# Chunked attention and a two-layer MLP in one kernel: the order of the transfers of tiles 1 to 5 and of tile 8 on SyncE's queue, and the general path's transfers on GpSimd's queue

## The chip, the cores and the metric

The kernel runs on one core of one Trainium2 chip. The metric is the device time of one execution in microseconds. Before the change it is 267.47 us, the median of three runs (267.15, 267.47 and 268.73). Engines are named as in the profile: PE (TensorE matmul), PEld (TensorE weight load), DVE (VectorE), ACT (ScalarE), POOL (GpSimd) and SP (SyncE, which issues nearly all transfers). "SPq" and "POOLq" are the instructions of an engine's sequencer that count as no work of the engine: issues of transfers, semaphore waits, branches.

## What is computed

Attention inside chunks of 64 keys, for 8 batches, 8 heads, 576 positions (9 chunks) and a head size of 64, and then an MLP on the result:

```python
scores = scale * np.matmul(q_c, k_c.transpose(0, 1, 2, 4, 3))     # per chunk of 64
attn = np.exp(scores - max); attn = attn / (sum(attn) + 1e-09)
x = np.matmul(attn, v_c)                # -> 4608 tokens x 512
h = x @ w_in                            # 512 x 2048
g = 0.5 * h * (1.0 + erf(h / sqrt(2)))
out = g @ w_out                         # 2048 x 512
```

Inputs and output are float32; the kernel multiplies in bfloat16.

## The kernel before

**Tiles.** The 4608 tokens are cut into nine tiles of 512. Tiles 0 to 7 hold the first eight chunks of one batch each, tile 8 the ninth chunk of all batches. The main loop `for t in range(1, NT)` runs the MLP of tile t on PE and beside it the attention of tile n = t + 1, the scores of tile t + 2 in part, and the transfers of tiles up to t + 3. Both matrix products use a seven-product scheme (four blocks by four, with sums and differences of blocks made by DVE): `mm1_seven` / `play` for the first (PE rows L598), `mm2_seven` (L758) and `mm2_steps` (L788) for the second.

**The way of an input.** A load (`load_qk`, `load_v_rows`; rows L136, L139, L142, L145, L152) brings float32 rows into a stage buffer ("arrival", six of them). A cast (rows L189, L193, L195, L235) writes them as bfloat16 to `q_nat`, `k_nat` or `v_nat`; nearly all casts run on POOL. For queries and keys a transposing transfer follows (`flip`, L228), which the scores need (`quad_S`, PE rows L261). V goes from the cast straight to `quad_av` (PE rows L346). So the chain is load, cast, flip, scores for q and k, and load, cast, `quad_av` for V.

**The way of an output.** PE sums one block of the second product in PSUM. `keep` copies a block to one of four `y` buffers (ACT, rows "kept L718" and "kept L795"), `done` adds to it (DVE, rows L723 and L798), and `store_block` (L863) sends it out: four stores of 256 KB for a tile. A `y` buffer comes free when its store has landed.

**What sets the order.** Each engine works its instructions off in program order, and that order is written out by hand (`manual_schedule`). For t = 1 the hooks `e1` and `e2` say after which piece of the tile's work a step is put: `e2[s]` stands ahead of piece s of the second product, which has 14 pieces (0 to 13). For t = 2, 3 and 4 the lists in `STEPS` say it, step by step: LQ, LK, LV are loads of q and k of tile t + 3 and of V of tile n + 1; CQ0 to CQ3, CK0 to CK3, CV the casts of these; FQ, FK the flips of tile n + 1; AV is `quad_av` of tile n; K1, K2, K3, K6 are `keep`s with K6 also storing; D1, D4, D5 are `done` with its store; XS1 to XS4 are DVE's sums of x, P0 to P3 DVE's partial row sums; s12 and the like are DVE's additions to products of the first layer. Q8, at the end of step list 4, loads and casts the queries of tile 8. For t of 5 and more `flip_qk(n + 1)` and `next_loads` stand at the head of the tile.

**SP at tile 1.** After the loads of q and k of tile 3 the program issues on SP, in this order: loads of q and k of tile 4 (`e2[4]`), the store of block (0,0) of tile 1, the flips of q and k of tile 3 and the nine loads of V of tile 3 (`e2[7]`), the stores of blocks (1,1), (0,1) and (1,0) of tile 1, and then the first flip of step list 2.

**The general path.** The fast path leaves out the maximum of the scores. DVE checks at the end that all row sums lie in a safe range (`range_test`, `range_count`, L891); each engine loads the count (L1332) and branches (L1333). If the count falls short, `general()` computes everything again, chunk by chunk, in a loop. In this input it is not taken. The instructions of L1358 are the program's end, where SP waits for all semaphores and the engines meet.

Of the kernel before, what the change touches and what calls it, by code (L numbers as in the profile page):

```python
# [11 lines left out]
def kernel(  # L12
# [9 lines left out]
    nc = tc.nc  # L22
# [5 lines left out]
    B, H, S, D = q.shape  # L28
# [154 lines left out]
    def cast_qk(t, nm, g, copy):  # L183
        st = tiles[t]
        if nm not in st:
            st[nm] = ld.tile([P, G, J, 2, D], bf16, tag="k", name="k_nat", bufs=3)
        if nm == "k" and t >= K0:
            for q0 in range(0, G, 2):
                copy(st[nm][:, q0:q0 + 2, g], st[nm + "f"][:, 2 * q0:2 * q0 + 4, g].rearrange("p (q r) d -> p q r d", r=2))  # L189
            return  # L190
        if t > T0:
            for j in range(0, J, 2):
                copy(st[nm][:, g, j:j + 2].rearrange("p j r d -> p r j d"), st[nm + "f"][:, 2 * g:2 * g + 2, j:j + 2])  # L193
            return
        copy(st[nm][:, g].rearrange("p j r d -> p r j d"), st[nm + "f"][:, 2 * g:2 * g + 2])  # L195
# [34 lines left out]
    def cast_v_rows(t, copy):  # L230
        st = tiles[t]
        st["v"] = ld.tile([P, H, CT // 2, D], bf16, tag="v", name="v_nat")
        for r in range(2):
            for n in range(CT // 2):
                copy(st["v"][:, r::2, n], st["vf"][:, r::2, n])  # L235
# [247 lines left out]
    def mm1_slot(t, f):  # L483
# [3 lines left out]
        for ks in range(KS):  # L487
# [32 lines left out]
             3: ('xs1', 'p1', "p1''", "p1'", 's11', 'FQ', "s11''", 'p2', "p2''", 'q5', 'xs2', "q5''", 'p6', "p6''", 'c11', 'k5', 'xs3', 'FK', 's12', "q5'", "c11''", "k5''", "s12''", "p1'''", 'p4', 'LQ', "p4''", "k5'", "s11'", 'c12', "c12''", 'xs4', 'p7', 'c22+', "s11'''", "p6'", "q5'''", 'LK', 'LV', 'c22', "p7''", "s12'", "c22+''", "k5'''", "p2'", "p7'", "p2'''", "p6'''", "c11'", "p4'", 'q3', "c22''", "c11'''", "c22+'", "c22'", "q3'", 'CQ0', "c12'", 'g3', "s12'''", "p7'''", "q3''", "g3'", "p4'''", 'CQ1', "c22+'''", "q3'''", "g3''", "c22'''", "c12'''", 'Y', "g3'''", 'S1a', 'S', 'Y', 'exp', 'CQ2', 'S3', 'E2', 'S1b', 'E0', 'S2b', 'Y', 'S2a', 'E1', 'Y', 'S4a', 'S4b', 'CQ3', 'E3', 'sums', 'K1', 't1', 'AV', 'Y', 'ov1', 'Y', 'CK0', 'Y', 'D1', 'ov0', 'R1', 'X1', 'K2', 'R0', 'ov3', 'Y', 'ov2', 'X0', 'K3', 'R3', 'XS1', 'X3', 'Y', 'Y', 'S+', 'E+3', 'Y', 'E+1', 'CK1', 'Y', 'R2', 'E+0', 'D4', 'X2', 'D5', 'CK2', 'CK3', 'P1', 'XS2', 'E+2', 'Y', 'P3', 'P2', 'CV', 'Y', 'gelu', 'XS4', 'K6', 'XS3', 'P0'),  # L520
             4: ("p1''", 'FQ', 'FK', "s11''", 'LQ', 'p1', "q5''", "p2''", 'LK', "p1'", 's11', "p6''", 'p2', "k5''", "s11'", "s12''", "p2'", "q5'", 'c11', 'q5', 'LV', "c11'", 'p6', "p6'", 'k5', "k5'", "p7''", "c11''", 's12', "p4''", "s12'", 'p7', "c22+''", "p7'", 'CQ0', "c12''", 'c22+', "p4'", 'p4', 'q3', "p1'''", "c22+'", "c22''", 'g3', "q3'", "q5'''", "s11'''", "g3'", "k5'''", 'CQ1', "p6'''", 'CQ2', 'Y', "c12'", 'T0', 'c22', "p2'''", "s12'''", 'R2', 'c12', "q3''", "c22'", "p7'''", "g3''", "p4'''", 'R1', 'Y', "c22+'''", 'R3', "c11'''", "c12'''", 'S1a', "q3'''", "c22'''", 'S1b', "g3'''", 'K1', 'AV', 'S2a', 'S2b', 'CQ3', 'CK0', 'S3', 'Y', 'Y', 'Y', 'Y', 'Y', 'Y', 'S4a', 'K2', 'Y', 'D1', 'Y', 'CK1', 'X3', 'K3', 'X2', 'X1', 'exp', 'CK2', 'X0', 'S+', 'S4b', 'Y', 'XS3', 'D4', 'E+0', 'CK3', 'E+2', 'E+3', 'E+1', 'XS1', 'gelu', 'Y', 'P0', 'XS2', 'Y', 'P2', 'Y', 'CV', 'D5', 'P3', 'XS4', 'P1', 'Q8', 'K6')}
# [286 lines left out]
    def play(t, order):  # L808
# [41 lines left out]
        does["FQ"], does["FK"] = lambda: flip(n + 1, "q"), lambda: flip(n + 1, "k")  # L850
        does["LV"], does["CV"] = lambda: load_v_rows(n + 1), lambda: cast_v_rows(n + 1, PO)
# [41 lines left out]
    def general():  # L893

        SUBS = mybir.AluOpType.subtract
        for c in range(4):
            n = d_ff // 4
            raw = stage_tile()[:].rearrange("p (ks n) -> p ks n", ks=KS)
            nc.sync.dma_start(raw, w_in_v[:, :, c * n:(c + 1) * n])
            DV(w_in_sb[:, :, c * n:(c + 1) * n], raw)  # L900
        for c in range(4):
            n = FF // 4
            raw = stage_tile()[:].rearrange("p (f n) -> p f n", f=n)
            nc.sync.dma_start(raw, w_out_v[:, c * n:(c + 1) * n, :])
            DV(w_out_sb[:, c * n:(c + 1) * n, :], raw)
# [4 lines left out]
    def one_chunk(b, s0, SUBS):  # L910
        rows = bass.ds(s0, CH)
        nat = {}
        for nm, src in (("q", q), ("k", k), ("v", v)):
            raw = stage_tile()[0:CH, 0:d_model]
            nc.sync.dma_start(raw.rearrange("p (h d) -> p h d", h=H),
# [54 lines left out]
        nc.sync.dma_start(by_batch[bass.ds(b, 1), rows].rearrange("o key d -> (o key) d"), y_sb[0:CH])  # L970
# [122 lines left out]
    with tc.manual_schedule():  # L1093
# [158 lines left out]
        for t in range(1, NT):  # L1252
# [26 lines left out]
            def next_loads():  # L1279
                if t + 3 == NT - 1:  # L1280
                    load_qk(t + 3, "k")
                    pool_cast_qk(t + 3, "k")
# [16 lines left out]
            if t <= T0:  # L1299
# [10 lines left out]
                if t == 1:  # L1310
# [4 lines left out]
                    e2[4].append(lambda: [load_qk(4, nm) for nm in "qk"])  # L1315
                    e2[7] += [lambda: pool_cast_qk(4), lambda: flip_qk(3), lambda: load_v_rows(3), lambda: cast_v_rows(3, PO)]
# [46 lines left out]
```

## Time and profile before

| | |
|---|---|
| median of three runs | 267.47 us |
| the profiled execution's own time | 269.52 us |
| its span, from the first to the last instruction | 267.7 us |
| mean granted TensorE clock | 0.993 |
| PE busy (share of the span) | 256.5 us (96%) |
| DVE busy | 223.3 us (83%) |
| ACT busy | 190.4 us (71%) |
| POOL busy | 104.7 us (39%) |
| transfers of SP's queue | 53.23 MB, 78.0% of 16 DMA engines' span |

The profiled execution took 2.05 us longer than the median run, and 1.8 us of its time lie outside the span. Rows of the timeline give start and length in us, the engine, the line, the operation, output and input, how many were merged into the row, and in brackets how long the engine had been idle and what ended that. Rows of the view by line give shortest, median and longest duration in ns.

### The profile page before, as it was taken

Reading aid. Unit: us, or ns where it says so; the run is one execution under the profiler, and the core shown is the slowest. Engines: PE = TensorE matmul, PEld = TensorE weight load, DVE = VectorE, ACT = ScalarE, POOL = GpSimd, SP = SyncE. Lnnn points to the kernel's source line nnn. Section 1 sums busy time; section 2 is a strip of 40 time slices with the busy share of each in tenths; the row PEclk is TensorE's granted clock in tenths of the full one; section 3 lists DMA queues with packets and bytes.
Section 4 is the critical chain, followed back from the end, with each engine's and each line's share of the span. In section 5 each row is a group of like instructions: output and inputs, shape, how many; then the busy total and the mean of one; then the engine's idle time right before and its main releaser. Section 6 shows DMA issues by size and latency. Waiting matters only on the chain.

```text
span 267.7 us, 7854 instructions
## 1 busy us (share of the span) xinstructions
PE 256.5 (96%) x3116; PEld 211.7 (79%) x3122; DVE 223.3 (83%) x397; ACT 190.4 (71%) x386; POOL 104.7 (39%) x229
## 2 busy tenths in 40 slices
PE   6599999999999999999999999999999999999992
PEld 2378865556888888887888888898888888888881
DVE  5767786998997687678999999999999999848771
ACT  3666667987767978898887588947894788237610
POOL 7778578702375370570390094087211300000000
PEclk9979999999999999999999999999999999999999
DMA  6999998979889999989999998999963310130014
GB/s 198 259 327 399 393 402 213 288 192 284 238 223 247 185 254 254 231 221 249 279 243 207 284 211 219 184 173 210 275 150 86 123 42 2 40 120 1 2 39 122
DMA packets 123415, 54.02 MB, mean 202 GB/s; under 512 B 97776, under 2 KB 120304, under 8 KB 123376
## 3 DMA queue, kind: packets, MB, share of 16 engines
q1 hardware_dynamic: 123072, 53.23, 78.0%
q8 instruction: 25, 0.41, 0.6%
q10 hardware_dynamic: 304, 0.26, 0.3%
q14 instruction: 14, 0.11, 0.1%
HBM read 36.70 MB, written 9.44 MB: 172 GB/s over the span
## 4 chain that ended last, share of the span: by engine, by line
PE 70%; ACT 8%; SPq 7%; DMA 6%; DVE 3%; POOL 2%; issue 2%; POOLq 0%; ACTq 0%
PE hs_ps L598 23%; PE y_ps L758 18%; PE y_ps L788 9%; PE h_ps L462 5%; ACT h L606 3%; DMA arrival<-in_q_dram 3%; SPq L152 3%; SPq L136 3%; PE y_ps L1021 3%; DMA arrival<-in_k_dram 2%; ACT k_bd L219 2%; PE h_ps L478 2%; PE av_ps L346 1%; DMA out_dram<-kept 1%; PE y_ps L985 1%
## 5 line engine op out<-in xcount | busy, mean ns | idle before, releaser
L606 ACT ACTIVATE h<-hs_ps 128x512 bf16<-128x512 f32 x87 | 49.7, 610 | 6.9 <-PE hs_ps L598 6.0
L235 POOL CAST v_nat<-arrival 128x256 bf16<-128x256 f32 x56 | 25.9, 488 | 37.3 <-DMA arrival<-in_v_dram 36.8
L598 PEld LDWEIGHTS <-w_in_sb 128*128 128x128 bf16 x348 | 33.9, 98 | 4.6 <-issue 0.2
L193 POOL CAST q_nat<-arrival 128x256 bf16<-128x256 f32 x40 | 17.9, 495 | 48.3 <-DMA arrival<-in_q_dram 26.8
L598 PE MATMUL hs_ps<-x,w_in_sb 128*128 128x256 bf16 x232 | 31.7, 272 | 0.0
L758 PEld LDWEIGHTS <-h 128*128 128x128 bf16 x240 | 23.2, 98 | 2.8
L1091 ACT ACT_TABLE_LOAD x16 | 20.5, 1283 | 1.0 <-PEq L1347 0.8
L718 ACT COPY kept<-y_ps 128x512 f32<-128x512 f32 (+1 forms) x17 | 9.0, 535 | 16.0 <-PE y_ps L758 13.0
L189 POOL CAST k_nat<-arrival 128x256 bf16<-128x256 f32 x48 | 18.6, 430 | 3.2 <-DMA arrival<-in_k_dram 3.2
L758 PE MATMUL y_ps<-w_out_sb,h 128*128 128x256 bf16 x160 | 18.6, 273 | 0.0
L758 PE MATMUL y_ps<-v_bd,k_bd 128*128 128x256 bf16 x160 | 18.5, 273 | 0.1
L758 PEld LDWEIGHTS <-k_bd 128*128 128x128 bf16 x160 | 15.6, 98 | 2.1 <-issue 0.2
L615 ACT COPY hs_ps<-hs_ps 128x512 f32<-128x512 f32 x29 | 16.2, 582 | 0.6 <-PE hs_ps L598 0.5
L598 PE MATMUL hs_ps<-k_bd,w_in_sb 128*128 128x256 bf16 x116 | 16.6, 273 | 0.0
L490 ACT ACTIVATE h<-h_ps 128x512 bf16<-128x512 f32 x21 | 12.5, 604 | 5.1 <-PE h_ps L462 3.6
L269 ACT ACTIVATE pT<-s_ps 128x512 bf16<-128x512 f32 x28 | 14.4, 599 | 1.8 <-PE s_ps L261 1.8
L788 PEld LDWEIGHTS <-h 128*128 128x128 bf16 x144 | 13.8, 98 | 1.7
L598 PE MATMUL hs_ps<-k_bd,w_in_more 128*128 128x256 bf16 x96 | 14.2, 273 | 0.0
L462 PE MATMUL h_ps<-x,w_in_sb 128*128 128x256 bf16 x128 | 14.2, 273 | 0.0
L598 PEld LDWEIGHTS <-w_in_more 128*128 128x128 bf16 x128 | 12.5, 98 | 2.0 <-issue 0.3
L723 DVE TENSOR_TENSOR kept<-y_ps,kept 128x512 f32<-128x512 f32 (+1 forms) x16 | 10.4, 651 | 4.0 <-PE y_ps L758 2.3
L462 PEld LDWEIGHTS <-w_in_sb 128*128 128x128 bf16 x128 | 12.4, 98 | 1.6 <-DVE w_in_sb L1066 0.2
(174 smaller groups left out, 640.2 us busy)
## 6 DMA issues: line engine op xcount, KB each, us to landing
arrival<-in_v_dram SPq DMA_DIRECT2D x58, 128.0 KB, 3.2
arrival<-in_k_dram SPq DMA_DIRECT2D x28, 256.0 KB, 5.8
arrival<-in_q_dram SPq DMA_DIRECT2D x7, 1024.0 KB, 6.7
out_dram<-kept SPq DMA_DIRECT2D x24, 256.0 KB, 3.1
arrival<-in_moe_w_out_dram SPq DMA_DIRECT2D x4, 1024.0 KB, 12.4
arrival<-in_moe_w_in_dram SPq DMA_DIRECT2D x6, 512.0 KB, 7.9
out_dram<-y_sb SPq DMA_DIRECT2D x8, 256.0 KB, 3.1
arrival<-in_v_dram SPq DMA_DIRECT2D x28, 64.0 KB, 2.8
```

The source lines that it names most:

```text
L189: copy(st[nm][:, q0:q0 + 2, g], st[nm + "f"][:, 2 * q0:2 * q0 + 4, g].rearrange("p (q r) d -> p q r d", r=2))
L193: copy(st[nm][:, g, j:j + 2].rearrange("p j r d -> p r j d"), st[nm + "f"][:, 2 * g:2 * g + 2, j:j + 2])
L235: copy(st["v"][:, r::2, n], st["vf"][:, r::2, n])
L269: nc.scalar.activation(pT[:].rearrange("p u (c j) -> p u c j", j=J), tiles[t]["s_ps"][m // 2][m % 2][:].rearrange("p u (j c) -> p u c j", ...
L462: nc.tensor.matmul(to[:, cols], left, right[:, cols], start=(start and a == 0), stop=stop, skip_group_check=True)
L490: nc.scalar.activation(tiles[t]["h"][:, f, :], h_ps[:], Act.Gelu)
L598: nc.tensor.matmul(hs[:, f], left[:, ks, f * P:(f + 1) * P], right[:, ks], start=(fresh and f == 0 and ks == 0), stop=(ks == 1), skip_grou ...
L606: nc.scalar.activation(h[:, n:n + HM, HD * c:HD * (c + 1)], src, Act.Gelu)
L615: "s11": lambda: AC(place_of("b")[:], bank["a"][:]),
L758: nc.tensor.matmul(to, left(f, m), right[:, f], start=(fresh and (split or m == 0) and f == 0), stop=(f == HF - 1), skip_group_check=True)
L788: nc.tensor.matmul(bank[name][:, m], left(f, m), right[:, f], start=(fresh and m == 0 and f == 0), stop=(f == HF - 1), skip_group_check=True)
L1091: nc.scalar.activation(act_scratch[:], rest[:, 0:1], func)
```

## The change

- **General path.** The loads and the store of `general` and `one_chunk` are issued by GpSimd's queue instead of SP's.
- **Tile 1.** `e2[4]` loads only the queries of tile 4; `e2[7]` casts only these. The flips of tile 3, the load and cast of the keys of tile 4 and the load and cast of V of tile 3 move to `e2[12]`, behind the stores of blocks (1,1) and (0,1) of tile 1.
- **V of tile 5.** The cast (CV) leaves the end of step list 3. A new step PV, fifth in step list 4, makes it, behind a one-element write of DVE to the same tile (`after=True`), so that POOL's casts wait for DVE to get there.
- **Queries of tile 8.** Q8 goes from the end of step list 4; for t = 5 `next_loads` brings q and k of tile 8 together.
- **Casts of k.** For tiles 2 and 3 each quarter is one cast of 128x512 instead of two of 128x256.

```diff
         if nm == "k" and t >= K0:
-            for q0 in range(0, G, 2):
-                copy(st[nm][:, q0:q0 + 2, g], st[nm + "f"][:, 2 * q0:2 * q0 + 4, g].rearrange("p (q r) d -> p q r d", r=2))
+            n = 2 if t > T0 else G
+            for q0 in range(0, G, n):
+                copy(st[nm][:, q0:q0 + n, g], st[nm + "f"][:, 2 * q0:2 * (q0 + n), g].rearrange("p (q r) d -> p q r d", r=2))
             return
...
-    def cast_v_rows(t, copy):
+    def cast_v_rows(t, copy, after=False):
         st = tiles[t]
         st["v"] = ld.tile([P, H, CT // 2, D], bf16, tag="v", name="v_nat")
+        if after:
+            nc.vector.memset(st["v"][0:1, 0:1, 0, 0:1], 0.0)
...
-             3: (... 'P3', 'P2', 'CV', 'Y', 'gelu', 'XS4', 'K6', 'XS3', 'P0'),
-             4: ("p1''", 'FQ', 'FK', "s11''", 'LQ', ... 'XS4', 'P1', 'Q8', 'K6')}
+             3: (... 'P3', 'P2', 'Y', 'gelu', 'XS4', 'K6', 'XS3', 'P0'),
+             4: ("p1''", 'FQ', 'FK', "s11''", 'PV', 'LQ', ... 'XS4', 'P1', 'K6')}
...
+        does["PV"] = lambda: cast_v_rows(n, PO, True)
...
-            nc.sync.dma_start(raw, w_in_v[:, :, c * n:(c + 1) * n])
+            nc.gpsimd.dma_start(raw, w_in_v[:, :, c * n:(c + 1) * n])
...
                 if t + 3 == NT - 1:
-                    load_qk(t + 3, "k")
-                    pool_cast_qk(t + 3, "k")
+                    bring_qk(t + 3)
...
-                    e2[4].append(lambda: [load_qk(4, nm) for nm in "qk"])
-                    e2[7] += [lambda: pool_cast_qk(4), lambda: flip_qk(3), lambda: load_v_rows(3), lambda: cast_v_rows(3, PO)]
+                    e2[4].append(lambda: load_qk(4, "q"))
+                    e2[7].append(lambda: pool_cast_qk(4, "q"))
+                    e2[12] = [lambda: flip_qk(3), lambda: load_qk(4, "k"), lambda: pool_cast_qk(4, "k"),
+                              lambda: load_v_rows(3), lambda: cast_v_rows(3, PO)]
```

The other three transfers of the general path (loads of `w_out` and of q, k, v, and the store) change in the same way as the one shown.

More of the change, by code (lines that the diff above doesn't have):

```diff
@@ L969, in one_chunk @@
         by_batch = out.rearrange("(b s) d -> b s d", s=S)
-        nc.sync.dma_start(by_batch[bass.ds(b, 1), rows].rearrange("o key d -> (o key) d"), y_sb[0:CH])
+        nc.gpsimd.dma_start(by_batch[bass.ds(b, 1), rows].rearrange("o key d -> (o key) d"), y_sb[0:CH])
     def last_piece(t, m, y_ps):
```

8 lines of the change are left out of this document (4 added, 4 removed).

## The prediction

> **What bounds the kernel now.** I read the busy times first, then PE's windows, then PE's waits.
>
> ```profile
> span 267.7 us, 7854 instructions
> PE 256.5 (96%) x3116; PEld 211.7 (79%) x3122; DVE 223.3 (83%) x397; ACT 190.4 (71%) x386; POOL 104.7 (39%) x229
> ...
> 20.00:263.00 243.00, 241.72 (x2961) 1.00 0.79 199
> ...
> PE y_ps L788 <- ACT kept L795: 0.2, 1, 0.2
> ```
>
> The window from 20 to 263 us holds 241.72 us of PE work in 243.00 us, at a granted clock of 1.00. PE idles there for 243.00 − 241.72 = 1.28 us, part of it after its last product. The only wait of PE on another engine in that stretch is the last row. The change takes no product away, so what lies between 20 and 263 us can give back about 1 us at most, whatever the transfers do. Two places are left: that one wait, and the end, where PE has nothing to do:
>
> ```profile
> 262.44 0.16 PE L890 MATMUL count<-small 128*1 128x1 bf16 x1
> 262.12 1.36 SPq L977 DMA_DIRECT2D out_dram<-y_sb  x2
> ...
> L1333 SPq EVENT_SEMAPHORE  x8: 17/17/17, 265.0 to 265.5; - x8
> L1333 POOLq COMPARE_BRANCH  x2: 38/42/45, 263.6 to 263.7; - x2
> ...
> L1333 SPq COMPARE_BRANCH  x2: 38/48/57, 264.6 to 265.5; - x2
> ...
> L1358 SPq EVENT_SEMAPHORE  x10: 17/28/28, 266.1 to 267.7; - x10
> L1358 POOLq EVENT_SEMAPHORE  x4: 17/17/17, 266.7 to 267.6; - x4
> ```
>
> From PE's end to the span's end 267.7 − 262.6 = 5.1 us pass. SP is the last engine there. At L1333, the branch past the general path, it handles eight semaphores one after the other between its two branches (264.6 and 265.5); POOL, whose part of the general path issues no transfer, has its two branches 0.1 us apart and no such rows. At 266.1 SP begins the closing waits, and POOL's first closing row (266.7) follows those.
>
> **The change part by part.**
>
> *General path on POOL's queue.* I read the eight semaphores as the bookkeeping of SP's transfers in the skipped block, one for each transfer semaphore. If they go with the transfers, SP's two branches come 0.1 us apart as POOL's do now, so 0.9 − 0.1 = 0.8 us fall away. SP's last store is issued by 262.12 + 1.36 = 263.5 us, and SP waits for it in any case; the first of the eight rows stands at 265.0, so I let SP reach the closing waits no sooner than about 265.3 instead of 266.1: still 0.8. Against that, new semaphores of POOL's queue will want closing waits too. SP's closing waits are among the ten rows of L1358; a step of that kind is priced by the eight of L1333, 0.5 us from first to last, 0.07 each. Four to eight more cost 0.3 to 0.5 us. POOL itself gets the eight steps: 263.7 + 0.6 = 264.3, two microseconds before its row at 266.7, so they are hidden by SP. The term is between −0.8 + 0.3 = −0.5 and −0.8 + 0.5 = −0.3 if both parts hold, −0.8 if no closing wait comes, and +0.5 if SP keeps its eight and the closing waits come on top. I take −0.5, since POOL's present rows are the nearest case of an engine without transfers in that block.
>
> [...]
>
> *Tile 1 on SP.* The rows of SP, PE, ACT, POOL and DVE that this touches:
>
> ```profile
> 75.08 1.36 SPq L142 DMA_DIRECT2D arrival<-in_q_dram  x1
> 76.49 7.27 SPq L136 DMA_DIRECT2D arrival<-in_k_dram  x4
> 83.86 0.79 SPq L863 DMA_DIRECT2D out_dram<-kept  x1
> 84.75 3.47 SPq L228 DMA_TRANSPOSE q_t<-q_nat  x1
> 88.33 2.79 SPq L228 DMA_TRANSPOSE k_t<-k_nat  x1
> 91.17 5.21 SPq L152 DMA_DIRECT2D arrival<-in_v_dram  x9
> 96.48 1.62 SPq L863 DMA_DIRECT2D out_dram<-kept  x2
> ...
> 79.07 0.68 DVE L723 TENSOR_TENSOR kept<-y_ps,kept 128x512 f32<-128x512 f32 x1
> ...
> 100.17 0.58 ACT L795 COPY kept<-y_ps 128x512 f32<-128x512 f32 x1 [1.90 <-DMA out_dram<-kept]
> 100.81 1.91 PE L788 MATMUL y_ps<-v_bd,s_sb 128*128 128x256 bf16 x16 [0.24 <-ACT kept L795]
> 102.64 0.71 PE L346 MATMUL av_ps<-pT,v_nat 64*64 64x64 bf16 x64
> ...
> 99.05 0.83 POOL L235 CAST v_nat<-arrival 128x256 bf16<-128x256 f32 x2 [0.35 <-DMA arrival<-in_v_dram]
> ```
>
> SP issues without a pause and far behind the program: the last `done` of tile 1 ends at 79.07 + 0.68 = 79.75 us, its store goes out after 96.48. ACT's K2 at 100.17 waited 1.90 us for such a store to land, and PE 0.24 us for K2. After the change two stores stand right behind the queries of tile 4, and the third behind them: 75.08 + 1.36 + 0.79 + 0.79 is 78.0 us, and the block (0,1) is ready at 79.75. SP waits 1.7 us there, with the flips of tile 3, the keys of tile 4, V of tile 3, the last store and, through the casts, POOL behind it. Both stores are out by 80.6 us, some 16 us earlier, so K2's buffer is free: PE gains 0.24 us.
>
> What becomes late is V of tile 3, now behind the keys. The same blocks stand ahead of it as before, plus two stores (1.62), plus the wait (1.7): at most 3.3 us. Its casts end at 99.05 + 0.83 = 99.88, and PE takes it at 102.64, so 2.76 us are free; at the full 3.3 PE would stall 0.5. But SP's rows for k are long because earlier transfers are still being worked off:
>
> ```profile
> 74.19 0.85 SPq L136
> ```
>
> One of the keys' four issues takes 0.85 us when nothing holds it, 3.4 for four, where the row above has 7.27. Time that SP waits comes back there. I take no stall, and keep 0 to +0.5 for the range. The flips of tile 3 move from 84.75 to about 80.6 and their scores only gain. At 98.7 SP begins step list 2 as before, since the sum of its work is unchanged, so what follows does not move.
>
> *V of tile 5.*
>
> ```profile
> 137.24 0.54 DVE L581 TENSOR_TENSOR k_bd<-x,k_bd 128x512 bf16<-128x512 bf16 x1
> 137.69 0.61 DVE L581 TENSOR_TENSOR k_bd<-x 128x512 bf16<-128x512 bf16 x1
> 79.67 0.41 DVE L581 TENSOR_TENSOR k_bd<-x 128x512 bf16<-128x512 bf16 x1
> ...
> 83.05 3.38 POOL L193 CAST q_nat<-arrival 128x256 bf16<-128x256 f32 x8 [3.60 <-DMA arrival<-in_q_dram]
> 137.10 2.84 POOL L235 CAST v_nat<-arrival 128x256 bf16<-128x256 f32 x7
> 140.42 0.40 POOL L235 CAST v_nat<-arrival 128x256 bf16<-128x256 f32 x1 [0.48 <-DMA arrival<-in_v_dram]
> 153.62 3.29 POOL L193 CAST q_nat<-arrival 128x256 bf16<-128x256 f32 x8 [12.80 <-DMA arrival<-in_q_dram]
> ...
> 139.30 0.70 DVE hs_ps L602
> 140.04 4.99 PE hs_ps L598 x44
> ...
> 148.96 0.64 PE av_ps L346 x64
> ```
>
> DVE's write stands between P0 and the addition at 139.30, so the casts start about 139.4 instead of 137.10, 2.3 us later, and end at 140.82 + 2.3 = 143.1. PE needs V at 148.96; behind the casts POOL has the queries of tile 7, which wait for their transfer until 153.62. Both covers are over 5 us. In return DVE's two sums at 137.24 and 137.69 lose POOL beside them: by the third row (0.41 at 79.67, while POOL idled for 3.60 us before 83.05) up to 0.13 + 0.20 = 0.33 us off DVE, against one small write. A write of one element has no row here; the bounds are 0 and the 0.41 of that sum. PE waits for DVE at 140.04 by some hundredths only, so this gives nothing forward and at worst +0.1. I take 0.
>
> *Queries of tile 8.*
>
> ```profile
> 163.43 3.93 SPq L145 DMA_DIRECT2D arrival<-in_q_dram  x8
> 167.45 0.40 SPq L863 DMA_DIRECT2D out_dram<-kept  x1
> 167.96 5.13 SPq L228 DMA_TRANSPOSE q_t<-q_nat  x1
> 173.19 3.16 SPq L228 DMA_TRANSPOSE k_t<-k_nat  x1
> ...
> 181.72 0.71 PE L261 MATMUL s_ps<-q_t,k_t 64*64 64x64 bf16 x64
> ```
>
> The eight loads move past one store and two flips. The flips of tile 7 start about 4 us sooner, and the scores that read them at 181.72 gain cover. The casts keep their place on POOL, and keys and V of tile 8 and 7 have the same work ahead as before. Zero. The merged casts of k are POOL and DVE work off PE's path: zero.
>
> *Sum.* −0.24 − 0.5 = −0.74 us on the profiled execution: 269.52 − 0.74 = 268.8, a span of 267.0. That execution stands 2.05 above the median of the runs, so the median goes from 267.47 to 266.7.
>
> **The rivals.**
>
> *The tail does not shrink.* SP keeps its eight steps, or the closing waits on POOL's new semaphores take as much as they free, up to +0.5. For it: the program's end waits for every semaphore. Against it: POOL's two bare branches. The time is 267.47 − 0.24 + (0 to 0.5) = 267.2 to 267.7; it is also what comes out if moving the general path does nothing at all. Chance 0.24.
>
> *The jump gets short too.* SP loses the 0.6 us from branch to L1358 as well: 266.7 − 0.6 = 266.1. [...] Chance 0.08.
>
> *V of tile 3 comes too late.* If nothing of the 7.27 us of the keys comes back, because the flips do not get forward while SP waits for the third store, the casts end at 99.88 + 7.27 = 107.15 and PE, in order, stands from 102.4 to there: 4.75 us. With the tail's −0.5 and PE's −0.24 that is 267.47 − 0.74 + 4.75 = 271.5, slower by 1.5%. It turns slower than before once V is 3.5 us late, and by over 1% at 6.2. For it: V's loads run behind four more large transfers. Against it: the flips that leave their place are 6.3 us long, and SP's rows were held by full queues. Chance 0.07.
>
> **How the numbers follow.** The forecast has the remaining 0.61 and a range of its own from 266.4 (−0.24 and −0.8, rounded) to 267.3 (the stall of 0.5 at tile 3 and the small terms). The runs of before scatter from 267.15 to 268.73, so a median may be off by a few tenths either way. For 8 in 10 I take the first two rivals in whole, with those tenths, and leave the third out: 265.8 to 268.3. About 1%, 2.7 us, is what a measurement of this kernel can tell from no change. Faster by that needs more than all idle time of PE and half the tail: 0.02. Slower by that is the last rival alone: 0.07. Within 1%: 0.91.
>
> **What would show it.** Right: PE's row for K2 gone and ACT's K2 without a wait; SP without the eight rows at L1333 and POOL with them; a tail of about 4.6 us from PE's last product. Stores (1,1) and (0,1) of tile 1 near 78 to 80 us. V of tile 5 cast from about 139.4. Wrong: a PE wait in front of L346 near 102 us on POOL's v_nat, a tail as long as 5.1 us or longer, or any new PE wait between 20 and 262 us.

## The result and the profile after

The changed kernel takes 267.23 us, the median of 22 runs (265.86 to 268.31), and the kernel before, timed beside it, 268.25 us (22 runs, 267.15 to 270.15). The ratio is 0.9952, with a 95% interval from 0.9937 to 0.9967, so the change takes off 268.25 x 0.0048 = 1.28 us (0.89 to 1.69); the two medians differ by 1.02. That is less than the 1% that the prediction took as what can be told from no change, and faster than before. The forecast was 266.7 us, from a change of −0.74 and a median of 267.47 over three runs. It is 0.5 us off, and two errors lean against each other in it: 22 runs put the kernel before 0.78 us higher, at 268.25, and the change gave 0.3 (by the medians) to 0.5 us (by the ratio) more than the sum. That the time came out this near is in part luck. Seven executions of the kernel before, timed beside the experiments on two of the chips below, were in a slower state, more than 1.5% above its fastest run there, and no ratio or median here counts them.

Two things outside the sum belong to every comparison here. The time outside the span is 1.57 us on average in the changed kernel and 1.82 in the kernel before (time of a run less its span, mean over the runs). And PE starts later. The first line of PE's waits that names `warm`, before and after:

```profile
PE warm L1080 <- DVE rest L47: 1.2, 1, 1.2
```

```profile
PE warm L1084 <- DVE rest L47: 1.4, 1, 1.4
...
PE s_ps L366 <- ACT k_bd L220: 0.9, 2, 0.6
...
PE tp L207 <- ACT k_bd L220: 0.2, 1, 0.2
```

The 0.23 us lost at the start and the 0.25 won outside the span cancel. Both stand in all runs that put the general path on GpSimd's queue, and in no other. In the list of after, four rows are left out, all on lines of tile 0 and the first stages like those shown: the wait on ACT's `kept` is gone. (Lines have moved by 1 to 5: L788 is L791 now, L795 is L798, L598 is L601, L602 is L605, L581 is L584, L228 is L229, L346 is L349, L235 is L238, L863 is L867, L1333 is L1338, L1358 is L1363.)

The page of the changed kernel (profiled execution 267.09 us) and its window over the stretch in which PE works:

```profile
span 265.5 us, 7854 instructions
...
PE 256.1 (96%) x3122; PEld 210.6 (79%) x3122; DVE 223.1 (84%) x394; ACT 190.5 (72%) x386; POOL 103.2 (39%) x225
```

```profile
20.00:261.50 241.50, 240.71 (x2953) 201.29 (x2951) 208.12 (x364) 178.73 (x367) 88.53 (x183) 1.00 0.78 200
```

PE is idle for 241.50 − 240.71 = 0.79 us between 20 and 261.5 us; it was 1.28 over the corresponding stretch. Busy times have hardly changed: what went is idle time and the tail.

**Where the two profiled spans part.** Both kernels load PE's weights 3122 times in one order, so the start of the n-th load in one trace less that in the other shows what has been won up to there:

| n-th weight load | 1 | 421 | 901 | 1101 | 1501 | 1701 | last | end of the span |
|---|---|---|---|---|---|---|---|---|
| start before, us | 1.20 | 48.58 | 93.18 | 103.14 | 130.71 | 149.01 | 262.44 | 267.7 |
| after less before, us | +0.23 | −0.72 | −0.72 | −1.12 | −1.12 | −1.29 | −1.29 | −2.19 |

There are four steps: −0.95 in the first 50 us, −0.40 at the second product of tile 1, −0.17 at the start of tile 4, and −0.90 behind PE's last load. The first step is not the change's. The windows of before and of after in the first stage (PEclk is the third figure from the end):

```profile
14.70:18.10 3.40, 3.40 (x44) 2.90 (x43) 2.52 (x7) 1.76 (x3) 2.83 (x7) 0.50 1.00 323
```

```profile
14.70:18.10 3.40, 3.14 (x56) 2.53 (x53) 2.31 (x5) 2.01 (x5) 2.77 (x7) 1.00 1.00 307
```

The profiled execution of before had the half clock for 3.4 us there. Another profiled execution of the changed kernel (e12, below) had it too, and the first stage was then 0.20 and not 0.72 us ahead. The half clock is not all of it: at the 421st load the other traces are ahead of before by 0.13 us (e10) to 1.79 (e2), and e4, whose edit does nothing so early, by 1.58. So of the 2.19 us between the two spans, the 0.7 won there are not put down to the change.

**The tail.** The rows by line of the branch past the general path, and of the program's end:

```profile
L1338 POOLq EVENT_SEMAPHORE  x4: 17/43/43, 262.5 to 262.7; - x4
...
L1338 SPq COMPARE_BRANCH  x2: 38/50/61, 263.3 to 263.4; - x2
...
L1338 POOLq INC_SWDGE_SEM  x1: 173/173/173, 262.8 to 262.8; - x1
```

```profile
L1363 SPq EVENT_SEMAPHORE  x14: 17/28/28, 263.9 to 265.5; - x14
L1363 POOLq EVENT_SEMAPHORE  x4: 17/17/17, 264.8 to 265.4; - x4
```

SP's eight rows are gone; its two branches are 0.1 us apart where they were 0.9. POOL has four rows and an INC_SWDGE_SEM of 0.17 us instead, done by 263.0. SP's closing rows are 14 where there were 10. They push POOL's first closing row from 0.6 us behind SP's first (266.1 to 266.7) to 0.9 (263.9 to 264.8). In return POOL's rows take 0.6 us from first to last where they took 0.9 (266.7 to 267.6). So the terms are −0.8, +0.3 and −0.3, and the rest of the tail's −0.9 is the rounding of the rows.

**Tile 1.** SP's timeline:

```profile
76.00 0.58 SPq L142 DMA_DIRECT2D arrival<-in_q_dram  x1
76.69 2.61 SPq L867 DMA_DIRECT2D out_dram<-kept  x3
79.39 5.47 SPq L229 DMA_TRANSPOSE q_t<-q_nat  x1
84.95 1.69 SPq L229 DMA_TRANSPOSE k_t<-k_nat  x1
86.70 4.70 SPq L136 DMA_DIRECT2D arrival<-in_k_dram  x4
91.44 6.95 SPq L152 DMA_DIRECT2D arrival<-in_v_dram  x9
```

The three stores are out by 79.3 us. POOL's, ACT's and PE's timelines of the same stage:

```profile
92.46 3.95 POOL L190 CAST k_nat<-arrival 128x256 bf16<-128x256 f32 x6 [1.29 <-DMA arrival<-in_k_dram]
96.36 4.38 POOL L238 CAST v_nat<-arrival 128x256 bf16<-128x256 f32 x8
```

```profile
97.58 0.59 ACT L798 COPY kept<-y_ps 128x512 f32<-128x512 f32 x1
```

```profile
97.92 1.92 PE L791 MATMUL y_ps<-v_bd,k_bd 128*128 128x256 bf16 x16
99.68 1.91 PE L791 MATMUL y_ps<-v_bd,s_sb 128*128 128x256 bf16 x16
101.52 0.71 PE L349 MATMUL av_ps<-pT,v_nat 64*64 64x64 bf16 x64
```

K2 no longer waits for a store, and PE goes from one L791 row to the next in 99.68 − 97.92 = 1.76 us. In before it took 100.81 − 98.64 = 2.17 us over the same two rows:

```profile
98.64 1.92 PE L788 MATMUL y_ps<-v_bd,k_bd 128*128 128x256 bf16 x16
```

So the wait cost 0.41 us, not the 0.24 in its bracket: a row's end is modelled and can lie behind the start of the next (97.92 + 1.92 = 99.84 against 99.68). V of tile 3 is cast at 96.36 + 4.38 = 100.74 and used at 101.52, with 0.78 us to spare where there were 2.76.

**V of tile 5.** POOL's and DVE's timelines:

```profile
138.12 2.81 POOL L238 CAST v_nat<-arrival 128x256 bf16<-128x256 f32 x8 [1.83 <-PE hs_ps L601]
```

```profile
136.03 0.54 DVE L584 TENSOR_TENSOR k_bd<-x,k_bd 128x512 bf16<-128x512 bf16 x1
136.49 0.41 DVE L584 TENSOR_TENSOR k_bd<-x 128x512 bf16<-128x512 bf16 x1
...
137.90 0.69 DVE L605 TENSOR_TENSOR hs_ps<-hs_ps,arrival 128x512 f32<-128x512 f32 x1
137.92 0.06 DVE L235 MEMSET v_nat<- 1x1 bf16 x1
```

The casts start at 138.12, behind the one-element write, which takes 0.06 us. The second of DVE's sums takes 0.41 where it took 0.61; the first still takes 0.54, since POOL's last cast of K runs into it (133.29 + 3.00 = 136.29). PE is 0.17 us further ahead after this stage. The queries of tile 8 (168.58 us on SP now) leave no mark on PE.

### The profile page after: what moved, and what is told of

Its sections match the earlier page's. It is cut to its first block, busy times and chain, and to the rows that moved or that the text cites. A ratio compares the mean times of both kernels' runs of the same rounds, so it can differ in the third digit from the quotient of the medians.

```text
span 265.5 us, 7854 instructions
## 1 busy us (share of the span) xinstructions
PE 256.1 (96%) x3122; PEld 210.6 (79%) x3122; DVE 223.1 (84%) x394; ACT 190.5 (72%) x386; POOL 103.2 (39%) x225
## 4 chain that ended last, share of the span: by engine, by line
PE 76%; DMA 10%; ACT 7%; SPq 4%; issue 1%; DVE 0%; POOL 0%
PE hs_ps L601 31%; PE y_ps L761 22%; PE y_ps L791 13%; DMA arrival<-in_moe_w_out_dram 8%; ACT h L609 3%; SPq L181 2%; PE h_ps L491 2%; DMA arrival<-in_moe_w_in_dram 2%; PE av_ps L349 2%; PE h_ps L481 2%; ACT pT L272 2%; SPq L142 1%; PE y_ps L1025 1%; PE y_ps L989 1%; PE s_ps L264 1%; ACT L1095 1%
## 5 line engine op out<-in xcount | busy, mean ns | idle before, releaser
L238 POOL CAST v_nat<-arrival 128x256 bf16<-128x256 f32 x56 | 24.9, 473 | 33.5 <-DMA arrival<-in_v_dram 23.1
L601 PEld LDWEIGHTS <-w_in_sb 128*128 128x128 bf16 x348 | 33.9, 98 | 4.7 <-issue 0.2
L194 POOL CAST q_nat<-arrival 128x256 bf16<-128x256 f32 x40 | 16.8, 467 | 50.2 <-DMA arrival<-in_k_dram 25.3
L601 PE MATMUL hs_ps<-x,w_in_sb 128*128 128x256 bf16 x232 | 31.8, 272 | 0.0
L190 POOL CAST k_nat<-arrival 128x256 bf16<-128x256 f32 (+1 forms) x44 | 19.1, 476 | 5.3 <-DMA arrival<-in_k_dram 5.3
L601 PE MATMUL hs_ps<-k_bd,w_in_sb 128*128 128x256 bf16 x116 | 16.6, 272 | 0.0
L791 PEld LDWEIGHTS <-h 128*128 128x128 bf16 x144 | 13.8, 98 | 1.7
L601 PE MATMUL hs_ps<-k_bd,w_in_more 128*128 128x256 bf16 x96 | 14.2, 273 | 0.0
L601 PEld LDWEIGHTS <-w_in_more 128*128 128x128 bf16 x128 | 12.5, 98 | 2.0 <-issue 0.3
```

Source lines behind the costliest of these rows:

```text
L190: copy(st[nm][:, q0:q0 + n, g], st[nm + "f"][:, 2 * q0:2 * (q0 + n), g].rearrange("p (q r) d -> p q r d", r=2))
L601: nc.tensor.matmul(hs[:, f], left[:, ks, f * P:(f + 1) * P], right[:, ks], start=(fresh and f == 0 and ks == 0), stop=(ks == 1), skip_grou ...
L791: nc.tensor.matmul(bank[name][:, m], left(f, m), right[:, f], start=(fresh and m == 0 and f == 0), stop=(f == HF - 1), skip_group_check=True)
```

## The experiments

Each row is one kernel. The tail is from the start of PE's last weight load to the end of the span, 5.30 us in the kernel before; the last column is the median of the kernel before on the same chip. The ratios of these medians differ from the ratios on record by up to 0.002 (e2: 0.9986, e9: 0.9983), which is within the intervals; e6 and e7 have four runs each.

| experiment | ratio to before (95%) | median, us | tail, us | before, us |
|---|---|---|---|---|
| e1_general_pool | 1.0019 (0.9986 to 1.0053) | 268.63 | 4.39 | 268.05 |
| e2_rest_only | 1.0004 (0.9979 to 1.0029) | 267.67 | 5.23 | 268.05 |
| e3_tile1_only | 1.0004 (0.9969 to 1.0039) | 268.10 | 5.29 | 268.05 |
| e4_v5_only | 1.0003 (0.9971 to 1.0035) | 268.16 | 5.29 | 268.05 |
| e5_general_act | 0.9991 (0.9955 to 1.0027) | 268.56 | 5.23 | 269.16 |
| e6_no_general | 0.9894 (0.9812 to 0.9976) | 266.37 | 3.63 | 269.16 |
| e7_v3_later | 1.0199 (1.0103 to 1.0294) | 274.86 | 4.40 | 269.16 |
| e8_pv_no_wait | 0.9934 (0.9896 to 0.9973) | 267.32 | 4.40 | 269.16 |
| e9_pool_and_v5 | 0.9965 (0.9935 to 0.9994) | 267.56 | 4.40 | 268.02 |
| e10_pool_and_tile1 | 0.9961 (0.9933 to 0.9989) | 266.99 | 4.40 | 268.02 |
| e11_general_pool_again | 0.9985 (0.9958 to 1.0013) | 267.78 | 4.40 | 268.02 |
| e12_changed_again | 0.9948 (0.9921 to 0.9975) | 266.86 | 4.39 | 268.02 |

### The general path alone: e1 and e11

The kernel before, with the four transfers of the general path on GpSimd's queue (one shown):

```diff
-            nc.sync.dma_start(raw, w_in_v[:, :, c * n:(c + 1) * n])
+            nc.gpsimd.dma_start(raw, w_in_v[:, :, c * n:(c + 1) * n])
```

> The kernel before, with the general path's four kinds of transfers on GpSimd's queue and nothing else changed. Theory (the tail is SP's bookkeeping of the skipped block): SP loses its eight rows between the two branches, POOL gains rows there, SP's closing waits grow from 8 to 12, and the time from PE's last weight load to the end of the span falls from 5.3 us to about 4.4 us; PE's wait for K2 (0.24 us near 100 us) stays. The median falls by 0.7 to 0.9 us, ratio about 0.997. Rival (the closing waits give it all back, or the gain of the changed kernel's tail was an accident of that execution): tail 5.1 us or more, ratio 1.000.

By-line rows of e1 at the branch and at the program's end:

```profile
L1333 POOLq EVENT_SEMAPHORE  x4: 17/43/43, 265.4 to 265.7; - x4
...
L1333 SPq COMPARE_BRANCH  x2: 38/50/61, 266.2 to 266.3; - x2
```

```profile
L1358 SPq EVENT_SEMAPHORE  x14: 17/28/28, 266.8 to 268.4; - x14
L1358 POOLq EVENT_SEMAPHORE  x4: 17/17/17, 267.7 to 268.4; - x4
```

The tail is that of the changed kernel, row by row, so this edit makes the whole of the tail's gain. The time did not follow: 1.0019. The profiled execution lost more elsewhere. DVE's, POOL's and PE's timelines of e1 between 132 and 142 us:

```profile
133.61 3.12 DVE L581 TENSOR_TENSOR k_bd<-x,k_bd 128x512 bf16<-128x512 bf16 x1
```

```profile
132.59 2.84 POOL L189 CAST k_nat<-arrival 128x256 bf16<-128x256 f32 x8
135.35 2.40 POOL L235 CAST v_nat<-arrival 128x256 bf16<-128x256 f32 x6
```

```profile
136.79 0.60 PE L598 MATMUL hs_ps<-k_bd,w_in_third 128*128 128x256 bf16 x4 [0.95 <-DVE k_bd L581]
...
141.49 0.60 PE L598 MATMUL hs_ps<-k_bd,w_in_third 128*128 128x256 bf16 x4 [1.45 <-DVE hs_ps L602]
```

A sum that takes 0.41 us when POOL is idle took 3.12 beside casts that POOL ran back to back, and PE waited 0.95 + 1.45 = 2.4 us for DVE. The first 135.43 − 133.61 = 1.8 us of it lie beside the casts of K, which the changed kernel has too; only the casts of V, beside the rest, are gone there. K2's stall was expected to stay, and it missed: ACT's K2 waited 1.04 us for a store in this execution, and PE not at all. So the kernel before pays this stall in some executions only.

This raised a question: does the general path on GpSimd's queue make such collisions frequent, and does the later cast of V of tile 5 take them away? e11 is the same kernel as e1 once more.

> The kernel before with only the general path on GpSimd's queue, once more. Its first run had the shorter tail (4.4 us) and yet no shorter time, and its profile shows one sum of x on DVE of 3.12 us instead of 0.4 beside POOL's casts near 134 us, and PE 2.4 us late behind it. Theory A (that stall comes by chance in some executions, here as in the kernel before, and the tail's gain is whole): ratio 0.995 to 0.997. Theory B (the stall is frequent as long as the casts of V of tile 5 follow those of the keys without a pause, and takes the gain back): ratio 0.999 to 1.003.

It came out at 0.9985, between the ranges of the two theories, the tail again 4.40, and no sum of x longer than 0.69 us in that stage. So this edit does not bring the collision each time. Whether it makes it more frequent, two traces can't show.

### The rest without the general path: e2

The changed kernel, with the four transfers back on SP:

```diff
-            nc.gpsimd.dma_start(raw, w_in_v[:, :, c * n:(c + 1) * n])
+            nc.sync.dma_start(raw, w_in_v[:, :, c * n:(c + 1) * n])
```

> The changed kernel with the general path's transfers back on SP's queue: only the transfers' order, the later cast of V of tile 5 and the merged casts are left. Theory: the tail is 5.2 to 5.4 us again with eight SP rows between the branches; ACT's K2 does not wait and PE has no wait on it; between the start of step list 2 and the last product PE gains 0.4 to 0.6 us against the kernel before. The median falls by 0.4 to 0.6 us, ratio about 0.998. Rival (the transfers' order is hidden anyway): nothing gained between those points, ratio 1.000.

The tail is the old one (5.23 us), the time outside the span 1.84, and PE's step at K2 is there (−0.40 between loads 901 and 1101). The time shows no gain: 1.0004, with an interval of ±0.0025, or ±0.7 us. The gain expected here is smaller than that, so the time neither shows nor excludes it.

### Tile 1 alone: e3

```diff
-                    e2[4].append(lambda: [load_qk(4, nm) for nm in "qk"])
-                    e2[7] += [lambda: pool_cast_qk(4), lambda: flip_qk(3), lambda: load_v_rows(3), lambda: cast_v_rows(3, PO)]
+                    e2[4].append(lambda: load_qk(4, "q"))
+                    e2[7].append(lambda: pool_cast_qk(4, "q"))
+                    e2[12] = [lambda: flip_qk(3), lambda: load_qk(4, "k"), lambda: pool_cast_qk(4, "k"),
+                              lambda: load_v_rows(3), lambda: cast_v_rows(3, PO)]
```

> The kernel before with only the new order of tile 1 on SP (stores of blocks (1,1) and (0,1) ahead of the flips, keys of tile 4 and V of tile 3). Theory: ACT's K2 near 98 us has no wait of 1.9 us and PE no gap of 0.24 us there; PE gains 0.2 to 0.4 us between the first products of step list 2 and those of step list 3; V of tile 3 is cast by 101.5 us, ahead of PE's use near 102 us, with no wait. Ratio 0.998 to 1.000. Rival (V of tile 3 too late): a PE wait on V near 102 us of 0.5 us or more, ratio above 1.000.

PE's step at K2 is −0.40 us, as in the whole change. POOL's and PE's timelines where V of tile 3 is needed:

```profile
96.81 4.46 POOL L235 CAST v_nat<-arrival 128x256 bf16<-128x256 f32 x8
```

```profile
101.67 0.71 PE L346 MATMUL av_ps<-pT,v_nat 64*64 64x64 bf16 x64
```

The casts end at 101.27, 0.40 us ahead of PE. So the edit spends nearly all of the 2.76 us that V of tile 3 had. The time is 1.0004: 0.4 us is below what ten runs tell.

### V of tile 5 alone: e4, and without its wait: e8

e4 is the kernel before with the later cast of V of tile 5; e8 is the changed kernel with the cast at the same place of the program, but without DVE's write.

```diff
-             3: (... 'P3', 'P2', 'CV', 'Y', 'gelu', 'XS4', 'K6', 'XS3', 'P0'),
-             4: ("p1''", 'FQ', 'FK', "s11''", 'LQ', ...
+             3: (... 'P3', 'P2', 'Y', 'gelu', 'XS4', 'K6', 'XS3', 'P0'),
+             4: ("p1''", 'FQ', 'FK', "s11''", 'PV', 'LQ', ...
+        does["PV"] = lambda: cast_v_rows(n, PO, True)
```

```diff
-        does["PV"] = lambda: cast_v_rows(n, PO, True)
+        does["PV"] = lambda: cast_v_rows(n, PO)
```

> The kernel before with only the cast of V of tile 5 moved behind DVE's one-element write in step list 4. Theory: POOL's casts of that V start at about 139.3 us instead of 137.1, DVE's two sums of x there take 0.41 and at most 0.54 us instead of 0.54 and 0.61, and PE's start of the products behind DVE's first addition of tile 4 moves forward by 0.1 to 0.2 us; nothing else moves. Ratio 0.999 to 1.000, not to be told from no change by time. Rival (DVE is not what PE waits for there): no shift of PE at all between tile 3 and tile 5.

> The changed kernel without DVE's one-element write ahead of the casts of V of tile 5: same place in the program, but POOL does not wait for DVE. Theory: the casts start as soon as the transfer is there, near 136 us, DVE's sums of x in that stretch take up to 0.6 us again, and PE is 0.1 to 0.2 us later behind DVE's first addition of tile 4. Ratio between this and the changed kernel not to be told from 1 by time. Rival (it is the place in the list that counts, not the wait): casts and sums as in the changed kernel.

In e4, PE gains 0.17 us between loads 1501 and 1701, as in the changed kernel. PE's waits of e4 still have the row of K2:

```profile
PE y_ps L790 <- ACT kept L797: 0.3, 1, 0.3
```

In e8 the casts of V run from 135.49 us, beside DVE's sums, and PE loses 0.08 us in that stage. So the later place in the program does not keep the casts away from the sums; DVE's write does, but for V alone. In e12, the changed kernel once more (below), the transfers came later, and POOL cast queries and keys beside the same two sums:

```profile
136.69 0.55 DVE L584 TENSOR_TENSOR k_bd<-x,k_bd 128x512 bf16<-128x512 bf16 x1
137.16 0.61 DVE L584 TENSOR_TENSOR k_bd<-x 128x512 bf16<-128x512 bf16 x1
...
134.46 3.04 POOL L194 CAST q_nat<-arrival 128x256 bf16<-128x256 f32 x8 [10.57 <-DMA arrival<-in_q_dram]
```

The sums take as long as in e8 (0.55 and 0.61), and PE loses 0.05 us. In these traces PE's gain goes with whether any casts run beside the second of the sums, and the write settles that only when the queries and keys are done by then. By time e4 (1.0003) and e8 (0.9934, beside 0.9952 and 0.9948 for the changed kernel) can't be told from no step.

### The general path on ACT's queue, and left out: e5 and e6

e5 is the changed kernel with the four transfers on ACT's queue. e6 has no general path: the load of the count, the branch and the block are left out, so it computes the fast path alone.

```diff
-            nc.gpsimd.dma_start(raw, w_in_v[:, :, c * n:(c + 1) * n])
+            nc.scalar.dma_start(raw, w_in_v[:, :, c * n:(c + 1) * n])
```

```diff
-        in_range = nc.values_load(total)
-        with tc.If(in_range < P, preferred_fallthrough_block=False):
-            general()
```

> The changed kernel with the general path's transfers on ACT's queue instead of GpSimd's. Theory (the bookkeeping goes with the engine that would issue): the eight rows between the branches appear on ACT, POOL and SP have bare branches, and SP's closing waits are 8 again instead of 12. ACT gets to its last row later than SP did, about 1.0 us behind its branch, so the tail is 4.3 to 4.9 us against 4.4 with GpSimd's queue: no gain over the changed kernel. Rival (any queue but SP's costs the same): the tail is 4.4 us and the rows are on none.

> The changed kernel without the general path: the range check still runs on DVE and PE, but no engine loads its result and there is no branch, so inputs outside the safe range would not be computed again. It measures how much of the tail the skipped block costs in all. Theory: SP reaches its closing waits right behind its last store's issue, these wait for the landing about 2.3 us after the issue, and the tail falls from 4.4 to about 3.5 us, set by the landing of the last stores plus eight closing waits (0.5 us) and the meeting of the engines (1.0 us). Ratio to before about 0.992. Rival (the landing of the last stores sets the tail already): 4.2 us or more.

By-line rows of e5 at the branch:

```profile
L1338 SPq EVENT_SEMAPHORE  x8: 17/17/17, 264.2 to 264.7; - x8
...
L1338 SPq COMPARE_BRANCH  x2: 38/48/57, 263.8 to 264.8; - x2
...
L1338 ACTq EVENT_SEMAPHORE  x1: 17/17/17, 263.9 to 263.9; - x1
```

This missed under both theories. SP has its eight rows although it issues nothing in the block, and ACT has one row as in every other kernel; the tail is 5.23 us. The time outside the span is longer too, 2.01 us. So the rows do not go with the engine that issues. In these runs transfers from SP and from ACT leave them on SP, transfers from GpSimd leave four on POOL. e6 shows what the block still costs: its tail is 3.63 us, 0.76 below that of the changed kernel. Among its by-line rows at the program's end, one of SP's seven closing rows is 0.38 us long instead of 0.03, which is read here as SP's wait for the last stores:

```profile
L1360 SPq EVENT_SEMAPHORE  x7: 17/28/383, 263.2 to 265.2; - x7
L1360 POOLq EVENT_SEMAPHORE  x4: 17/17/17, 264.6 to 265.2; - x4
```

### V of tile 3 later still: e7

The changed kernel with the loads and casts of V of tile 3 behind the flips of step list 2. This brings about what the third rival foretold, V of tile 3 too late, and prices it.

```diff
-                              lambda: load_v_rows(3), lambda: cast_v_rows(3, PO)]
+    STEPS = {2: (... 'W3.2', 'p2', 'FK', 'V3', "p2''", ...
+        does["V3"] = lambda: [load_v_rows(3), cast_v_rows(3, PO)]
```

> The changed kernel with the loads and casts of V of tile 3 moved on once more, behind both flips of tile 4 in step list 2. It measures the price of that V coming late, which the changed kernel escapes by under a microsecond. Theory: the loads start near 98.5 us instead of 91.4, the casts end near 107 us instead of 100.7, PE takes V as soon as they end and waits some 5 to 6 us at its use near 101.6 us; none of it comes back later, since PE is busy all the time. Ratio 1.015 to 1.02 against before. Rival (the transfers have slack and V still comes early): PE's wait there is under 1 us, ratio below 1.000.

PE's waits, PE's timeline and the windows of e7:

```profile
PE av_ps L349 <- POOL v_nat L238: 5.6, 2, 4.4
```

```profile
98.77 1.91 PE L791 MATMUL y_ps<-v_bd,s_sb 128*128 128x256 bf16 x16
101.88 0.21 PE L349 MATMUL av_ps<-pT,v_nat 64*64 64x64 bf16 x1 [1.21 <-POOL v_nat L238]
106.47 1.06 PE L349 MATMUL av_ps<-pT,v_nat 64*64 64x64 bf16 x63 [4.38 <-POOL v_nat L238]
107.47 3.60 PE L791 MATMUL y_ps<-w_out_sb,s 128*128 128x256 bf16 x16
```

```profile
98.00:105.00 7.00, 2.89 (x26) 2.26 (x23) 2.88 (x5) 5.30 (x19) 2.54 (x7) 1.00 0.95 215
105.00:112.00 7.00, 5.53 (x85) 4.19 (x86) 4.68 (x8) 0.00 (x0) 2.72 (x9) 0.51 1.04 268
```

PE waits 1.21 + 4.38 = 5.6 us. It loses 8.0 us against before between loads 901 and 1301, because the clock is halved from 105 to 112 us: the same 16 products take 3.60 us at 107.47 and 1.91 at 98.77. The price of a late V is its wait and some 2.4 us more, 2.8 against the changed kernel, which is 0.40 us ahead over the same loads.

### Pairs of parts, and the whole again: e9, e10 and e12

e9 is e1's edit with e4's, e10 is e1's edit with e3's, and e12 is the changed kernel once more. All three were timed beside e11.

```diff
-            nc.sync.dma_start(raw, w_in_v[:, :, c * n:(c + 1) * n])
+            nc.gpsimd.dma_start(raw, w_in_v[:, :, c * n:(c + 1) * n])
+        does["PV"] = lambda: cast_v_rows(n, PO, True)
```

```diff
-            nc.sync.dma_start(raw, w_in_v[:, :, c * n:(c + 1) * n])
+            nc.gpsimd.dma_start(raw, w_in_v[:, :, c * n:(c + 1) * n])
+                    e2[12] = [lambda: flip_qk(3), lambda: load_qk(4, "k"), lambda: pool_cast_qk(4, "k"),
+                              lambda: load_v_rows(3), lambda: cast_v_rows(3, PO)]
```

> General path on GpSimd's queue and the later cast of V of tile 5, nothing else. Theory A: as the general path alone, 0.995 to 0.997 both. Theory B: better than the general path alone by 0.003 or more, and no sum of x on DVE over 1 us between 130 and 140 us in its profile.

> General path on GpSimd's queue and the new order of tile 1, nothing else. Theory A: 0.994 to 0.997, with ACT's K2 not waiting. Theory B: as the general path alone plus at most the 0.4 us of K2, 0.998 to 1.002. If this one alone is better by 0.003 or more than the general path alone, then the order of tile 1 and not V of tile 5 makes the difference.

> The changed kernel once more, on one chip with the three that follow. First theory: ratio to before 0.994 to 0.997; tail 4.4 us and 1.55 us outside the span, against 5.3 and 1.82.

The whole comes out again, 0.9948. The mean spans on this chip are 266.39 us for before, 266.18 with the general path alone, 265.88 with V of tile 5 too, 265.74 with tile 1 in its stead, and 265.40 for all. The order is that of a sum of parts, though neighbours are within each other's intervals. ACT's K2 does not wait in e10, as expected. e9 has no sum of DVE over 0.7 us between 132 and 139 us, but it is only 0.002 faster than e11 (0.001 by the medians), less than the 0.003 that was asked for, and e10, which leaves V of tile 5 where it was, is as fast. So it is not shown that the later cast of V of tile 5 is what makes the general path's gain visible, though it lies in the right direction.

### The two small steps over all traces

Each trace is one execution, so the two steps are read over all of them, in the way of the table of the first section: what PE gains (−) or loses against the kernel before.

| step | kernels | us |
|---|---|---|
| loads 901 to 1101 (K2) | tile 1 in the new order: after, e2, e3, e5, e8, e12; e10; e6 | −0.40 in each of six; −0.34; −0.18 |
| | tile 1 in the old order: before, e4, e11, e1, e9 | 0; +0.09; −0.21; −0.40; −0.40 |
| loads 1501 to 1701 (V of tile 5) | with DVE's write: after, e4, e5, e9; e7, e2, e12, e6 | −0.17 in each of four; −0.11; −0.06; +0.05; +0.28 |
| | without it: before, e8, e3, e11, e10, e1 | 0; +0.08; +0.11; +0.20; +0.26; +2.49 |

The new order of tile 1 is worth 0.37 − 0.18 = 0.2 us by the means (e7, which stalls there, left out). Read from start to start of the two rows at K2, the step is cleaner: 1.75 or 1.76 us in all nine traces with the new order, and in the old order 2.25 (e4), 2.17 (before), 1.94 (e11) and 1.75 (e1 and e9), with ACT's K2 waiting 1.99, 1.90, 1.68, 1.04 and 0.97 us for a store. So a wait of ACT of about 1 us cost PE nothing here, and the mean gain is 1.97 − 1.76 = 0.2 again.

The later cast of V of tile 5 is worth 0.16 + 0.14 = 0.3 us by the middles of the two rows, an estimate from few traces. The second of DVE's sums tells the traces apart better than the edit does: it takes 0.41 or 0.42 us with no cast beside it in after, e4, e5, e9 and e7, and 0.61 beside casts of queries and keys in e2, e12 and e6, the three with the write that gain less or lose. e10's 0.26 is lost from 146 us on, behind the last casts of V, so not all of the lower row is due to casts. e1's 2.49 is in the row without the write, but more than half of its collision lay beside casts of K.

## Why the prediction was right, and where its sizes were off

**What bounds the kernel.** Right. PE's busy time is the same to 0.4 us, and all that could be won lay in PE's idle time and the tail.

**The tail** (predicted −0.5, measured −0.9). The mechanism was right: SP's eight rows go, the time between its branches falls by 0.8 us, and four closing waits come on top, the lower end of "four to eight", for +0.3. (Eight of them at 0.07 us would have cost 0.6, not the upper 0.5 of the sum.) e1 and e11 show that this edit alone does it, and e2 that the rest does none of it. Two things were off. POOL's own closing rows became 0.3 us shorter (0.9 to 0.6), a term that the sum did not have, so that the whole 0.8 remained. It is 0.7 in e1 and 0.6 in e6, and 0.9 in e2, e5 and before; what makes it is open. And the reading that gave the edit its price, "If they go with the transfers", held for GpSimd only: e5 moved the transfers to ACT, and the rows stayed on SP. By the same reading ACT's queue would have been given the same gain, and e5's tail has none of it.

**K2's stall** (predicted −0.24, measured −0.40 between the two traces). Right in place and cause: e3 has the step, and e4, without the edit, has the stall. The size was read from the bracket, which is idle time behind a modelled end; from start to start of the same two rows it is 0.41. But PE's stall is there in some executions only: e1 and e9 leave tile 1 as it was and don't have it, though ACT waits in both. Over all traces the edit is worth 0.2 us, by chance near the value that the bracket gave.

**V of tile 3** (predicted 0, bounds 0 to +0.5). Right: no stall. The slack that the prediction worked out, 2.76 less at most 3.3, came to 0.78 in the changed kernel and 0.40 in e3. SP's keys did take less time (7.27 us before, 4.70 after), as the reason that was given would have it. How full the queues were no run shows; the DMA share over those rows was higher in after, 1.10 (86.70 to 91.40 us) against 0.94 (76.49 to 83.76).

**V of tile 5** (predicted 0, at worst +0.1). Mis-sized: −0.17 between the two traces, and 0.3 by the middles of all traces. DVE's relief was foreseen, and was said to give "nothing forward" since PE waited for DVE by hundredths only. As at K2, the idle time in front of PE's row made the wait look too small: PE gained 0.22 us at DVE's additions, between loads 1601 and 1621. And the relief depends on the execution: it came in five of the eight traces with the write, and stayed out in the three in which POOL cast queries and keys at that moment. In one trace without the write, e1, the collision was far larger than the prediction's bounds for these sums.

**The start and the end outside the span** were not in the sum. They are worth +0.23 and −0.25 and come with GpSimd's queue; PE's first wait is 1.4 us in e7 and e8 also, and 1.2 in e2, e3, e4, e5 and e6.

**The sum by its measured terms** is −0.9 for the tail, −0.2 for K2, −0.3 for V of tile 5, +0.23 and −0.25: −1.4 us. The time shows −1.28 (−0.89 to −1.69). The prediction's −0.74 lies outside that interval, and the two terms that were too small, the tail by 0.4 and V of tile 5 by 0.3, make up more than the difference. The terms come from single traces and the times from many runs, so that they meet is no proof of the split.

**The rivals.** The tail shrank, so the first falls. The second took SP's 0.6 us from its last branch to L1358 as saved, and with it the range's lower end of 265.8; no run shows that they can be saved. SP's way from its last branch to the closing waits is 0.5 us in after (263.4 to 263.9) and in e5 (264.8 to 265.3), as it was before within the rows' rounding. POOL's way from its last branch to its first row at the program's end, 0.1 us in before (263.7 to 263.8), grew to 0.4 in after (263.1 to 263.5), when POOL's part of the block got the transfers. Why SP's did not shrink in turn, no run shows. The third did not come; e7 shows that it would have cost what was said and more.

**What stays open.** The general path alone has 0.9 us off its tail in two traces, and its time shows none of it in one set of runs (1.0019) and less than half in the other (0.9985, or −0.4 us). e1's execution shows where it can go, a collision of DVE and POOL; e11's does not. Stalls of this size come and go from execution to execution in many of the kernels here: the 3.4 us of half clock in the first stage, DVE's sum of 3.12 us, a sum at L694 near 118 us that takes 1.61 us in e10 and 0.68 in e11. Whether the general path's move makes any of them more frequent was not settled. So the tail's 0.9 us are shown in the traces, and how much of them reaches the time is not. The merged casts of k have no run of their own; in after they stand at 55 to 57 and at 77 to 79 us, and PE's lead is 0.72 us both ahead of them and behind (loads 421 and 901), so they leave no mark on PE there.

## What to carry to other kernels

A block that is never taken still has a price (0.76 us of the tail in the changed kernel, by e6), and it is read from the semaphore rows at its branch and at the program's end, not from its transfers: here the kind of queue used in the block decided 0.9 us of the tail. Before trusting who will carry such rows, look for a case of each candidate, since two queues that look alike may share them, as here: with the transfers on ACT's queue the eight rows stayed on SP (e5). Price a short stall from start to start of the rows around it (0.41 us at K2, 0.24 by the bracket), and against several executions, since a trace shows one meeting of two engines, and the next execution may show another (a sum of 3.12 us in e1, 0.69 in e11).

## What the runs showed of the hardware

**In e7 the clock was halved around a long wait of PE.** PE stood still for 4.38 us (102.1 to 106.5), and the granted clock was 0.51 from 105 to 112 us, with 1.00 from 98 to 105 and from 112 to 120. If it was either full or half there, as in the first stage of before (0.50 for 3.4 us, 1.00 on both sides), that makes 7 x 0.49 / 0.50 = 6.9 us at half, about twice those 3.4 us (an estimate from these windows). It then fell by 105.1, while PE was still waiting, and PE worked at half clock for about 5.4 us. That the wait brought the fall is read from their meeting, in one execution. The waits of up to 1.45 us in e1 brought no half clock in that stage (1.00 from 133 to 149 us).

**In e1 a vector sum took 3.12 us beside casts on GpSimd.** It reads two tiles, and such a sum took 0.42 with POOL idle (80.12 us in before, 79.56 in after), so it took 2.7 us more, as long as some seven of the casts beside it (2.84 / 8 = 0.36 us each). The casts were not held up: the eight of K took 2.84 us there, and 3.00 to 3.02 in before, after and e9, where the same sum took 0.51, 0.42 and 0.63 beside them. In e11 that sum took 0.69. That the casts held the sum up is read from their meeting and was not tested; it was seen in one execution and not in the repeat.
